# Long-row transposing DMAs with strided reads, a scale moved into the drive term, and a busier TensorE at the start

## The chip, the cores and the metric

The kernel runs on one core of one Trainium2 chip. The metric is the device time of that core in microseconds, from runs without a profile unless it is said otherwise. A run more than 1.5% above the fastest of the same kernel is called slow.

## The reference

The input is x and f_logit of shape (4, 6144, 256) and a `lower_bound` of 256 numbers. A gated recurrence runs along the tokens of each of the 4 sequences, and a maxout layer follows on all 24,576 tokens.

```python
sig = 1.0 / (1.0 + np.exp(-f_logit))
f = lower_bound + (1.0 - lower_bound) * sig
i = 1.0 - f
for t in range(S):
    h = f[:, t] * h + i[:, t] * x[:, t]
    y[:, t] = h
# y as (24576, 256); w1, w2: (256, 1024); w_out: (1024, 256)
out = np.maximum(y @ w1, y @ w2) @ w_out
```

The kernel uses max(a, b) = a + relu(b - a): it multiplies y by wd = w2 - w1 (1024 wide), applies a Relu, multiplies by w_out, and adds y times the fused matrix w13 = w1 @ w_out. Numbers are bf16 in SBUF.

## The kernel before

Tokens are worked on in blocks of 512 (48 blocks). For the recurrence, channels lie on partitions (two halves, KC = 2) and tokens along the free dimension. From the fifth chunk on (chunks of 1024 tokens = 2 blocks) the input is cast to bf16 into a DRAM scratch by GpSimd's DMA queue, and a transposing DMA on SP's queue brings it into SBUF:

```python
    def cross(c):
        nt = chunks[c][2]
        for s in range(2):                       # s = 0: f_logit, s = 1: x
            if by_xbar(c, s):                    # c >= 4
                dst = inpool.tile([P, KC, CH], BF16, name=("fT", "xT")[s])
                nc.sync.dma_start_transpose(
                    out=dst[:, :, 0:nt], in_=held[c, s][0:nt, :]
                )
                held[c, s] = dst
```

The gate runs on ACT (ScalarE): u = sigmoid(-f_logit). The rest of the recurrence runs on DVE (VectorE), in the order of this list (shortened: allocations and the lookup of the inputs are left out):

```python
    def gate(j):                                 # ACT
        nc.scalar.activation(out=like(u[:, :, 0:nb], fT), in_=fT,
                             func=AF.Sigmoid, scale=-1.0)

    def scan_steps(j):                           # DVE
        def decay(h):                            # ff = 1 - (1 - lower_bound) * u
            nc.vector.tensor_scalar(out=ff[:, h, 0:nb], in0=u[:, h, 0:nb],
                scalar1=nom[:, h : h + 1], scalar2=1.0, op0=ALU.mult, op1=ALU.add)
        def drive():                             # v = u * x; its factor om is folded into wd and w13
            nc.vector.tensor_tensor(out=like(v[:, :, 0:nb], xT),
                in0=like(u[:, :, 0:nb], xT), in1=xT, op=ALU.mult)
        def scan(h):                             # y[t] = ff[t] * y[t-1] + v[t]
            nc.vector.tensor_tensor_scan(out=y[:, h, 0:nb], data0=ff[:, h, 0:nb],
                data1=v[:, h, 0:nb], initial=init, op0=ALU.mult, op1=ALU.add)
        return [lambda: decay(0), lambda: decay(1), drive, lambda: scan(0), lambda: scan(1)]
```

The main loop interleaves the work of three neighbouring blocks. In the traces ACT and DVE run their instructions in the order in which they are issued here:

```python
        for j in range(2, NBLK + 1):
            ...
            gates = {}
            if j + 1 < NBLK and by_xbar(blocks[j + 1][3], 0):
                gates[0] = j + 1                 # gate of the NEXT block, after this block's first Relu
            if j + 2 < NBLK and not by_xbar(blocks[j + 2][3], 0):
                gates[FC // 2] = j + 2
            ...
            for fc in range(FC):                 # FC = 8
                if j < NBLK:
                    first_layer(j, fc)           # PE: 2 matmuls 128x512; ACT: Relu out of PSUM
                if j > 2:
                    second_layer(j - 1, fc)      # PE: 5 matmuls 128x256; at fc = 3 and 7 DVE evicts osb<-psO
                ...
                if fc in gates:
                    gate(gates[fc])
                if fc == 0 and 2 < j < NBLK - 1:
                    scans = scan_steps(j + 1)
                if fc < len(scans):
                    scans[fc]()
```

## Time and profile before

| | |
|---|---|
| time, median of the first 3 runs | 400.97 us (400.66 to 401.63) |
| span of the profiled run | 428.3 us, a slow run (430.05 us) |
| TensorE per block of 512 tokens, unstalled | 7.82 us |

These lines are from the page of before: the span, the busy time of each engine, TensorE's and DMA's busy tenths in 40 slices of the span (PE is TensorE, PEld its loading of weights, POOL is GpSimd), the DMA queue of SP (packets, MB, share of 16 engines' time), and the two lines of the chain that ended last.

```profile
span 428.3 us, 6970 instructions
PE 392.8 (92%) x2744; PEld 296.8 (69%) x2792; DVE 248.7 (58%) x359; ACT 268.5 (63%) x447; POOL 26.4 (6%) x58
...
PE   3999979798789999998997899999998999999996
...
DMA  7999999999999999999998999999999999998112
...
q1 hardware_dynamic: 100512, 51.13, 66.7%
...
PE 46%; DMA 34%; SPq 15%; ACT 3%; DVE 1%; issue 1%; ACTq 0%
PE psO L410 25%; DMA fT<-scr_0_90 20%; PE dT L381 19%; SPq L153 13%; DMA fT<-scr_1_91 12%; ACT u L190 2%; DMA w1n_110<-in_moe_w_dram 2%; SPq L433 1%; PE psO L352 1%; ACT rt L389 1%; PE tT L180 1%; PE psO L365 0%; SPq L121 0%; DVE osb L430 0%; DVE y L233 0%
```

In this slow run DMA is busy throughout and the chain runs through transposing DMAs. Between their stalls the blocks follow each other every 7.82 us (start of the first Relu of each block), and the stalls add up to 28.1 us. Without them the span is 400.2 us. The fast timed runs of before in the later rounds have spans of 398.6 to 400.2 us (a time is 1.8 us longer than its span). So fast runs should be bound by TensorE.

The three groups that the change touches, from the list of groups by line with shapes (busy us, mean ns of one | idle of the engine before, and who ended it):

```profile
L190 ACT ACTIVATE u<-fT 128x1024 bf16<-128x1024 bf16 x44 | 46.4, 1054 | 35.5 <-DMA fT<-scr_1_91 18.2 <-DMA fT<-scr_0_90 17.3
L220 DVE TENSOR_TENSOR v<-u,xT 128x1024 bf16<-128x1024 bf16 x44 | 30.3, 688 | 3.8 <-DMA xT<-scr_0_92 1.8 <-DMA xT<-scr_1_93 1.7
L209 DVE TENSOR_SCALAR ff<-u,nom 128x512 bf16<-128x512 bf16 x94 | 29.0, 351 | 105.0 <-ACT u L190 105.0
```

And one unstalled block of the recurrence, from the timeline of before (start us, duration us, and in brackets how long the engine had been idle and on whom it waited):

```profile
141.53 1.05 ACT L190 ACTIVATE u<-fT 128x1024 bf16<-128x1024 bf16 x1
...
142.62 0.62 DVE L209 TENSOR_SCALAR ff<-u,nom 128x512 bf16<-128x512 bf16 x2 [1.38 <-ACT u L190]
143.15 0.69 DVE L220 TENSOR_TENSOR v<-u,xT 128x1024 bf16<-128x1024 bf16 x1
...
144.46 0.69 DVE L430 COPY osb<-psO 128x512 f32<-128x512 f32 x1 [0.62 <-PE psO L410]
...
145.06 2.45 DVE L233 TENSOR_TENSOR_SCAN y<-ff,y,v 128x512 bf16<-128x512 bf16 x2
```

Gate, decay, drive and scans stand one behind the other, with an eviction of the output (`osb`, a copy out of PSUM) between drive and scans. DVE is idle twice in this block.

### The profile page before, as it was taken

The numbers are of one execution on the slowest core, as the hardware profiler recorded it, in microseconds if no ns is written. First come the engines' busy times: TensorE is split into PE (matmuls) and PEld (weight loads), VectorE is DVE, ScalarE is ACT, GpSimd is POOL, SyncE is SP. The second block draws the span as 40 slices with busy tenths as digits, with TensorE's granted clock in tenths as the row PEclk, the third lists the DMA queues.
The fourth block names the chain that finished last, engine by engine and source line by source line (L and its number), as shares of the span: only waits on it lengthen the run. The fifth ranks groups of instructions, "written<-read, shape, count | busy, mean of one in ns | idle before, by whom it ended". The sixth has DMA issues, their size and how long they took to land.

```text
span 428.3 us, 6970 instructions
## 1 busy us (share of the span) xinstructions
PE 392.8 (92%) x2744; PEld 296.8 (69%) x2792; DVE 248.7 (58%) x359; ACT 268.5 (63%) x447; POOL 26.4 (6%) x58
## 2 busy tenths in 40 slices
PE   3999979798789999998997899999998999999996
PEld 1677756576557777776775577767676777777775
DVE  5785637455357566564653557657547656567551
ACT  3656656557366676675673666756657676776762
POOL 1400000000000000000000000000000000000000
PEclk9999999999989999999999699999999999999999
DMA  7999999999999999999998999999999999998112
GB/s 245 222 220 198 123 157 141 137 169 252 81 240 226 119 239 233 112 248 168 183 237 75 218 158 186 250 145 170 219 131 231 226 216 164 268 157 179 79 69 100
DMA packets 103377, 77.01 MB, mean 180 GB/s; under 512 B 93552, under 2 KB 94064, under 8 KB 102640
## 3 DMA queue, kind: packets, MB, share of 16 engines
q1 hardware_dynamic: 100512, 51.13, 66.7%
q0 software_dynamic: 2544, 25.17, 36.1%
q8 instruction: 22, 0.36, 0.4%
q10 hardware_dynamic: 288, 0.26, 0.2%
q14 instruction: 11, 0.09, 0.1%
HBM read 53.48 MB, written 48.23 MB: 237 GB/s over the span
## 4 chain that ended last, share of the span: by engine, by line
PE 46%; DMA 34%; SPq 15%; ACT 3%; DVE 1%; issue 1%; ACTq 0%
PE psO L410 25%; DMA fT<-scr_0_90 20%; PE dT L381 19%; SPq L153 13%; DMA fT<-scr_1_91 12%; ACT u L190 2%; DMA w1n_110<-in_moe_w_dram 2%; SPq L433 1%; PE psO L352 1%; ACT rt L389 1%; PE tT L180 1%; PE psO L365 0%; SPq L121 0%; DVE osb L430 0%; DVE y L233 0%
## 5 line engine op out<-in xcount | busy, mean ns | idle before, releaser
L389 ACT ACTIVATE rt<-dT 128x512 bf16<-128x512 f32 x384 | 219.2, 598 | 104.1 <-PE dT L381 100.0
L381 PE MATMUL dT<-y,wd 128*128 128x512 bf16 x720 | 219.5, 384 | 21.3 <-ACT rt L389 19.5
L410 PE MATMUL psO<-wob,rt 128*128 128x256 bf16 x1536 | 230.7, 274 | 2.7 <-issue 0.4
L410 PEld LDWEIGHTS <-rt 128*128 128x128 bf16 x1536 | 170.7, 114 | 41.4 <-issue 1.1
L233 DVE TENSOR_TENSOR_SCAN y<-ff,y,v 128x512 bf16<-128x512 bf16 x88 | 107.9, 1268 | 0.1
L430 DVE COPY osb<-psO 128x512 f32<-128x512 f32 x94 | 64.7, 690 | 59.0 <-PE psO L410 58.9
L381 PEld LDWEIGHTS <-wd 128*128 128x128 bf16 x768 | 75.8, 99 | 33.2 <-issue 24.6
L209 DVE TENSOR_SCALAR ff<-u,nom 128x512 bf16<-128x512 bf16 x94 | 29.0, 351 | 105.0 <-ACT u L190 105.0
L410 PE MATMUL psO<-w_109,y 128*128 128x256 bf16 x384 | 74.0, 275 | 0.0
L410 PEld LDWEIGHTS <-y 128*128 128x128 bf16 x384 | 43.4, 113 | 42.6 <-issue 3.5
L190 ACT ACTIVATE u<-fT 128x1024 bf16<-128x1024 bf16 x44 | 46.4, 1054 | 35.5 <-DMA fT<-scr_1_91 18.2
L220 DVE TENSOR_TENSOR v<-u,xT 128x1024 bf16<-128x1024 bf16 x44 | 30.3, 688 | 3.8 <-DMA xT<-scr_0_92 1.8
L98 POOL DMA_DIRECT2D scr_0_90<-in_f_logit_dram x11 | 5.4, 493 | 149.7 <-DMA fT<-scr_0_90 149.7
L98 POOL DMA_DIRECT2D scr_1_91<-in_f_logit_dram x11 | 5.3, 486 | 148.8 <-DMA fT<-scr_1_91 148.1
L233 DVE TENSOR_TENSOR_SCAN y<-ff,v 128x512 bf16<-128x512 bf16 x6 | 7.0, 1208 | 0.0
L98 POOL DMA_DIRECT2D scr_0_92<-in_x_dram x11 | 5.4, 488 | 18.7 <-DMA xT<-scr_0_92 16.9
L98 POOL DMA_DIRECT2D scr_1_93<-in_x_dram x11 | 5.3, 486 | 15.7 <-DMA xT<-scr_1_93 14.9
L190 ACT ACTIVATE u<-tT 128x1024 bf16<-128x1024 bf16 x3 | 3.2, 1058 | 4.3 <-PE tT L180 4.3
L352 PE MATMUL psO<-ident_f,w1n_110 128*128 128x128 f32 x8 | 1.9, 422 | 3.4 <-DMA w1n_110<-in_moe_w_dram 3.4
L341 ACT ACTIVATE wd<-wdf,om 128x128 bf16<-128x128 f32 (+1 forms) x6 | 2.2, 428 | 4.3 <-DVE wdf L333 4.3
L352 PEld LDWEIGHTS psO<-ident_f,w1n_110 128*128 128x128 f32 x8 | 1.6, 221 | 3.7 <-issue 3.7
L220 DVE TENSOR_TENSOR v<-u,tT 128x1024 bf16<-128x1024 bf16 x3 | 3.6, 1216 | 0.0
(49 smaller groups left out, 45.1 us busy)
## 6 DMA issues: line engine op xcount, KB each, us to landing
out_dram<-osb SPq DMA_DIRECT2D x47, 512.0 KB, 4.8
scr_0_90<-in_f_logit_dram POOLq DMA_DIRECT2D x11, 512.0 KB, 7.5
scr_0_92<-in_x_dram POOLq DMA_DIRECT2D x11, 512.0 KB, 12.4
scr_1_91<-in_f_logit_dram POOLq DMA_DIRECT2D x11, 512.0 KB, 7.9
scr_1_93<-in_x_dram POOLq DMA_DIRECT2D x11, 512.0 KB, 13.6
fn<-in_f_logit_dram POOLq DMA_DIRECT2D x3, 256.0 KB, 7.9
xn<-in_x_dram POOLq DMA_DIRECT2D x3, 256.0 KB, 8.6
w2n_112<-in_moe_w_dram SPq DMA_DIRECT2D x1, 512.0 KB, 6.5
```

Source lines behind the costliest of these rows:

```text
L98: nc.gpsimd.dma_start(out=scr[0:nt, :].rearrange("(p i) d -> p (i d)", p=P), in_=src.rearrange("(p i) d -> p (i d)", p=P),)
L153: nc.sync.dma_start_transpose(out=dst[:, :, 0:nt], in_=held[c, s][0:nt, :])
L180: nc.tensor.transpose(dst, src, ident[:])
L190: nc.scalar.activation(out=like(u[:, :, 0:nb], fT), in_=fT, func=AF.Sigmoid, scale=-1.0)
L209: nc.vector.tensor_scalar(out=ff[:, h, 0:nb], in0=u[:, h, 0:nb], scalar1=nom[:, h : h + 1], scalar2=1.0, op0=ALU.mult, op1=ALU.add,)
L220: nc.vector.tensor_tensor(out=like(v[:, :, 0:nb], xT), in0=like(u[:, :, 0:nb], xT), in1=xT, op=ALU.mult,)
L233: nc.vector.tensor_tensor_scan(out=y[:, h, 0:nb], data0=ff[:, h, 0:nb], data1=v[:, h, 0:nb], initial=init, op0=ALU.mult, op1=ALU.add,)
L352: nc.tensor.transpose(pt[:, kc, q, :], half(w1n, g)[:, kc, 2 * r + q], ident_f[:])
L381: nc.tensor.matmul(dT[:, 0:nb], lhsT=wd[:, kc, fc * P : (fc + 1) * P], rhs=y[:, kc, 0:nb], start=(kc == 0), stop=(kc == KC - 1),)
L389: nc.scalar.activation(out=rt[:, 0:nb], in_=dT[:, 0:nb], func=AF.Relu)
L410: nc.tensor.matmul(ps[:, r, :], lhsT=left, rhs=right, start=(s == 0 and (r == 0 or j == NBLK - 1)), stop=(s == n - 1 and (r == 1 or j == N ...
L430: nc.vector.tensor_copy(out=osb[:, 2 * g : 2 * g + 2, :], in_=ps[:])
```

## The change

The intent: give the transposing DMAs 16 long rows (64 consecutive tokens each, 32 KB) instead of 1024 short ones, to make them cheaper. The price is that the tokens land interleaved: token 64 r + i lies at place i, sub-place r, so gate and drive read one token every 64 bytes. The scale om moves from the weights into the drive term, which saves work before the first matmul, and idle transposes are to keep TensorE's clock up at the start.

```diff
@@ cross, turn_steps
-                dst = inpool.tile([P, KC, CH], BF16, name=("fT", "xT")[s])
+                dst = inpool.tile([P, CH // XR * KC, XR], BF16, name=("fT", "xT")[s])
+                ni = nt // XR                                   # XR = 16
                 nc.sync.dma_start_transpose(
-                    out=dst[:, :, 0:nt], in_=held[c, s][0:nt, :]
-                )
-                held[c, s] = dst
+                    out=dst[:, 0 : ni * KC, :],
+                    in_=held[c, s][0:nt, :].rearrange("(r i) d -> r (i d)", r=XR),
+                )
+                held[c, s] = dst[:, 0 : ni * KC, :].rearrange(
+                    "p (i k) r -> p k r i", k=KC
+                )
...
-                turned[j, s] = held[c, s][:, :, o : o + nb]
+                ni = chunks[c][2] // XR
+                turned[j, s] = held[c, s][:, :, o // ni : (o + nb) // ni, :]
@@ the drive (also in the first recurrence)
+    def scaled_product(v, u, xT):
+        for h in range(KC):
+            nc.vector.scalar_tensor_tensor(
+                out=v[:, h], in0=u[:, h], scalar=om[:, h : h + 1], in1=xT[:, h],
+                op0=ALU.mult, op1=ALU.mult,
+            )
...
-            nc.vector.tensor_tensor(out=like(v[:, :, 0:nb], xT), in0=like(u[:, :, 0:nb], xT), in1=xT, op=ALU.mult)
+            scaled_product(like(v[:, :, 0:nb], xT), like(u[:, :, 0:nb], xT), xT)
@@ the weights: wd = w2 - w1 in one DVE subtract; om is no longer multiplied in
-        for kc in range(KC):
-            (nc.scalar.mul or nc.vector.tensor_scalar_mul of wdf by om)      # shortened
@@ the start
-        for q in range(8):
-            nc.tensor.transpose(wt[:, 0:P], ident[:], ident[:])
+        keep_busy(20)
...
         first_turn(1)
+        keep_busy(28)
         first_recurrence(1)
...   (first layer of block 0 before the transposes of w1; two w1T copies go to ACT)
```

More of the change, by code (lines that the diff above doesn't have):

```diff
@@ L38 @@
     CH = 1024
+    XR = 16
     assert S % CH == 0
@@ L197, in like @@
             return t
-        return t.rearrange("p k (m i) -> p k m i", m=P)
+        return t.rearrange("p k (m i) -> p k m i", m=src.shape[2])
+    def scaled_product(v, u, xT):
+        for h in range(KC):
+            nc.vector.scalar_tensor_tensor(
+                out=v[:, h],
+                in0=u[:, h],
+                scalar=om[:, h : h + 1],
+                in1=xT[:, h],
+                op0=ALU.mult,
+                op1=ALU.mult,
+            )
     def scan_steps(j):
@@ L219, in drive @@
             xT = turned[j, 1]
-            nc.vector.tensor_tensor(
-                out=like(v[:, :, 0:nb], xT),
-                in0=like(u[:, :, 0:nb], xT),
-                in1=xT,
-                op=ALU.mult,
-            )
+            scaled_product(like(v[:, :, 0:nb], xT), like(u[:, :, 0:nb], xT), xT)
         def scan(h):
@@ L272, in first_recurrence @@
             )
-        nc.vector.tensor_tensor(
-            out=like(v[:, :, cols], xT), in0=like(u[:, :, cols], xT), in1=xT,
-            op=ALU.mult,
-        )
+        scaled_product(like(v[:, :, cols], xT), like(u[:, :, cols], xT), xT)
         for h in range(KC):
@@ L300 @@
     wob = wpool.tile([P, FC, D], BF16)
-    wdf = wpool.tile([P, KC, DFF], FP32)
     wd = wpool.tile([P, KC, DFF], BF16)
@@ L333, in make_wd @@
         nc.vector.tensor_tensor(
-            out=wdf[:, :, cols].rearrange("p kc (q m) -> p kc q m", q=n),
+            out=wd[:, :, cols].rearrange("p kc (q m) -> p kc q m", q=n),
             in0=half(w2n, g)[:, :, qs],
@@ L338, in make_wd @@
         )
-        for kc in range(KC):
-            if g == 0:
-                nc.scalar.mul(wd[:, kc, cols], wdf[:, kc, cols], om[:, kc : kc + 1])
-            else:
-                nc.vector.tensor_scalar_mul(
-                    out=wd[:, kc, cols], in0=wdf[:, kc, cols], scalar1=om[:, kc : kc + 1]
-                )
     def turn_w1(k):
@@ L355, in turn_w1, with keep_w1T @@
         return pt
-    def keep_w1T(k, pt):
+    def keep_w1T(k, pt, copy):
         dst = w1T[:, 2 * k : 2 * k + 2, :].rearrange("p q (k d) -> p k q d", k=KC)
-        nc.vector.tensor_copy(out=dst, in_=pt[:])
+        copy(out=dst, in_=pt[:])
     def make_w13():
@@ L371, in make_w13, with keep_busy @@
                 )
-            nc.scalar.mul(w13[:, kc, :], psw[:, 0, :], om[:, kc : kc + 1])
+            nc.scalar.copy(out=w13[:, kc, :], in_=psw[:, 0, :])
+    def keep_busy(n):
+        wt = ps_d.tile([P, TB], BF16, name="dT")
+        for q in range(n):
+            nc.tensor.transpose(wt[:, 0:P], ident[:], ident[:])
     rts = {}
@@ L465 @@
         nc.scalar.activation(out=warm[:], in_=om[:, 0:1], func=AF.Sigmoid)
-        wt = ps_d.tile([P, TB], BF16, name="dT")
-        for q in range(8):
-            nc.tensor.transpose(wt[:, 0:P], ident[:], ident[:])
+        keep_busy(20)
         first_bf16(0, 0, nc.vector.tensor_copy)
@@ L479 @@
         make_wd(2, 2)
+        for fc in range(0, 4):
+            first_layer(0, fc)
         pts = [turn_w1(0), turn_w1(1)]
-        for fc in range(2):
+        make_wd(4, 2)
+        make_wd(6, 2)
+        for fc in range(4, 6):
             first_layer(0, fc)
         for k in range(2):
-            keep_w1T(k, pts[k])
-        for fc in range(2, 4):
+            keep_w1T(k, pts[k], nc.scalar.copy)
+        for fc in range(6, 8):
             first_layer(0, fc)
-        make_wd(4, 2)
-        make_wd(6, 2)
         pts = [turn_w1(2), turn_w1(3)]
-        for fc in range(4, 8):
-            first_layer(0, fc)
         for k in range(2):
-            keep_w1T(2 + k, pts[k])
+            keep_w1T(2 + k, pts[k], nc.vector.tensor_copy)
         make_w13()
```

## The prediction

> **What bounds the kernel now.** TensorE, from about 40 us on. In the timeline an unstalled block of 512 tokens takes 7.82 us (eight times two 128x512 matmuls and five 128x256, 0.977 us). ACT needs 8 x 0.60 + 1.05 = 5.9 us of it, DVE 2 x 0.35 + 0.69 + 2 x 1.27 + 2 x 0.69 = 5.3 us. The page's span, 428.3 us, is not the timed 401: the profiled run was a slow one. Its blocks lose 28.1 us to stalls, in which the gate waited for a transposed fT (list of waits: ACT from DMA fT 35.5 us); transposes and stores keep SP's queue full and the DMA row reads 9. 428.3 - 28.1 = 400.2 us, within 1 us of the timed median. So I believe that timed runs hardly stall: about 40.7 us of start, 45 blocks at 7.82, 8 us of end.
>
> **What the change does.**
> 1. Transposes from 16 rows of 32 KB. Today each has 2048 packets of 256 B (median 18 ns, mean 35 ns) and holds SP's queue 7 to 8 us, 2.2 at least. I expect fewer or cheaper packets and shorter issues. This takes away the profiled stalls (page span 400 to 410 us), but nearly nothing of the timed 401.
> 2. Reads with a stride of 64 B in gate and drive. The Trainium skill ("SBUF - State Buffer", note on cachelines) says that each access to a new 16-byte line pays a penalty; no read here shows it. Strided PSUM reads by the gate cost nothing (1058 ns against 1054). I estimate the gate at 1.05 to 1.9 us.
> 3. Drive as two scalar_tensor_tensor. The PSUM-fed drive takes 1.22 us for 1024 elements, so I estimate 2 x 0.62 us against 0.69: DVE 5.9 of 7.82 us. The scan ends 1.6 us before the next block and DVE waits 0.6 us for an eviction between drive and scans, which hides it. Not on the chain.
> 4. Start. wd needs one DVE subtract, no scaling: first matmul at about 11.8 instead of 12.93 us. The clock was half until 17.1 us ("TensorE: Matmul & The Clock Gate", Part 1: about 3.4 us of sustained work release it; the trace agrees: half clock from 119.5 to 122.9 us after a 4 us stall). Warm, 8 matmuls at 213 instead of 427 ns save 1.7 us of PE. But Relus (0.51 to 0.60 us each), the weights' landing (about 13.7 us), two w1T copies now in ACT's order (0.6 us each) and two on DVE (0.65 us) then decide when the fused weight matrix is done: by hand 20.8 us instead of 21.26. So 0.5 of a possible 2.5 us reaches the chain; the recurrences of blocks 1 and 2 follow unchanged.
>
> **Prediction.** 400.2 us, 397.5 to 402.5; faster by over 2%: 0.06, within 2%: 0.88, slower: 0.06.
>
> **What would show it.** Right: blocks 7.82 us apart; ACT's wait for DMA fT under 10 us; transposes issued in 2 to 4 us; drive near 2 x 0.62 us; block 0's first-layer matmuls 0.22 us apart, but block 3's first Relu still near 40 us. Wrong in step 1: transposes as long, or more packets. Wrong in step 4: block 3 before 39 us.
>
> **What would make it wrong.** Strided SBUF reads costing three times a plain one: DVE passes 7.82 us a block (slower). Transposes that read rows 32 KB apart more slowly, so that DMA bounds timed runs too. Or timed runs that do stall on DMA today behind a shorter start, which I cannot see; then the gain is 3 to 8 us.

## The result, and the profile after

| | before | after |
|---|---|---|
| time, median | 401.3 us of 4 runs, one of them slow (435.82) | 435.74 us of 4 runs (434.5 to 436.8) |
| ratio of fast runs | | 1.0863 (1.082 to 1.0905) |
| block to block | 7.82 us | 8.60 us |
| block 3's first Relu | 40.74 us (slow profile) | 40.95 us |

A ratio is the mean time of one kernel's fast runs over that of the other's in the same rounds, so not quite the ratio of the medians quoted. The changed kernel is 8.6% slower. Its loss is even: from block 3 to block 47 there are 44 steps of 8.60 instead of 7.82 us, 34.1 us in all, against 34.4 us between the medians.

The same lines of the page of after:

```profile
span 434.5 us, 7093 instructions
PE 396.6 (91%) x2784; PEld 298.9 (69%) x2832; DVE 301.1 (69%) x402; ACT 300.9 (69%) x443; POOL 26.6 (6%) x58
...
PE   6899998999899999989998999899989989998996
...
DMA  7998987897878679778788579798788877551212
...
q1 hardware_dynamic: 11104, 51.13, 40.0%
...
DVE 55%; ACT 21%; PE 12%; issue 8%; DMA 2%; SPq 1%; ACTq 0%; DVEq 0%
DVE y L245 24%; DVE v L208 20%; ACT u L196 20%; PE dT L387 7%; DVE osb L436 6%; PE psO L416 4%; DVE ff L226 4%; DMA w1n<-in_moe_w_dram 2%; ACT rt L395 2%; PE tT L186 1%; SPq L122 0%; PE psO L353 0%; DVE w1T L360 0%; PE psO L366 0%; ACTq L39
```

SP's queue has 11,104 packets instead of 100,512, and ACT does not wait for a transposed tile (what of this is owed to the state of before's profile, e8 below tells). But the chain has moved to DVE and ACT, though neither is busy for more than 69% of the span. That is the mark of a loop of latencies: no engine is full, and yet each waits for the one before. The groups:

```profile
L196 ACT ACTIVATE u<-fT 128x1024 bf16<-128x1024 bf16 x44 | 85.7, 1949 | 0.0
L208 DVE SCALAR_TENSOR_TENSOR v<-u,om,xT 128x512 bf16<-128x512 bf16 x88 | 92.5, 1093 | 0.0
L226 DVE TENSOR_SCALAR ff<-u,nom 128x512 bf16<-128x512 bf16 x94 | 29.0, 350 | 112.1 <-ACT u L196 112.1
```

The gate went from 1054 to 1949 ns, and the drive from one instruction of 688 ns to two of 1093 ns. The decay, whose operands are still contiguous, stayed. The chain of waits of after for one block, in order of time (start us, us, what):

```profile
170.47 1.94 ACT u L196
172.41 0.03 issue
172.44 0.04 DVE ff L226
172.48 0.23 issue
172.71 0.35 DVE ff L226
173.05 2.02 DVE v L208 x2
175.07 0.60 DVE osb L436
175.67 2.38 DVE y L245 x2
178.05 0.04 issue
178.09 0.39 PE dT L387
...
178.56 0.06 ACT rt L395
178.62 0.43 issue
179.06 1.95 ACT u L196
```

It closes on itself after 179.06 - 170.47 = 8.59 us. The gate of block j+1 stands in ACT's order behind the first Relu of block j; that Relu needs a matmul, which needs y of block j, whose scans need the drive and decay of block j, which need the gate of block j. Every term of this sum is a latency that all others wait for.

### The profile page after: what moved, and what is told of

It reads as the page before. It is cut to its first block, busy times and chain, and to the rows that moved or that the text cites. A ratio compares the mean times of both kernels' runs of the same rounds, so it can differ in the third digit from the quotient of the medians.

```text
span 434.5 us, 7093 instructions
## 1 busy us (share of the span) xinstructions
PE 396.6 (91%) x2784; PEld 298.9 (69%) x2832; DVE 301.1 (69%) x402; ACT 300.9 (69%) x443; POOL 26.6 (6%) x58
## 3 DMA queue, kind: packets, MB, share of 16 engines
q1 hardware_dynamic: 11104, 51.13, 40.0%
## 4 chain that ended last, share of the span: by engine, by line
DVE 55%; ACT 21%; PE 12%; issue 8%; DMA 2%; SPq 1%; ACTq 0%; DVEq 0%
DVE y L245 24%; DVE v L208 20%; ACT u L196 20%; PE dT L387 7%; DVE osb L436 6%; PE psO L416 4%; DVE ff L226 4%; DMA w1n<-in_moe_w_dram 2%; ACT rt L395 2%; PE tT L186 1%; SPq L122 0%; PE psO L353 0%; DVE w1T L360 0%; PE psO L366 0%; ACTq L395 0%
## 5 line engine op out<-in xcount | busy, mean ns | idle before, releaser
L387 PE MATMUL dT<-y,wd 128*128 128x512 bf16 x720 | 224.2, 382 | 28.4 <-DVE y L245 27.1
L208 DVE SCALAR_TENSOR_TENSOR v<-u,om,xT 128x512 bf16<-128x512 bf16 x88 | 92.5, 1093 | 0.0
L196 ACT ACTIVATE u<-fT 128x1024 bf16<-128x1024 bf16 x44 | 85.7, 1949 | 0.0
L387 PEld LDWEIGHTS <-wd 128*128 128x128 bf16 x768 | 75.2, 98 | 11.8 <-issue 2.5
L416 PE MATMUL psO<-w,y 128*128 128x256 bf16 x384 | 73.2, 272 | 0.0
L99 POOL DMA_DIRECT2D scr<-in_f_logit_dram x22 | 10.8, 490 | 286.1 <-DMA fT<-scr 285.4
L99 POOL DMA_DIRECT2D scr<-in_x_dram x22 | 10.7, 487 | 37.6 <-DMA xT<-scr 35.3
L378 PE MATMUL dT<-ident 128*128 128x128 bf16 x48 | 5.5, 314 | 1.6 <-DVE ident L455 1.6
L378 PEld LDWEIGHTS <-ident 128*128 128x128 bf16 x48 | 5.1, 150 | 1.6 <-DVE ident L455 1.6
L208 DVE SCALAR_TENSOR_TENSOR v<-u,om,tT 128x512 bf16<-128x512 bf16 (+1 forms) x10 | 5.9, 637 | 0.2 <-PE tT L142 0.2
L341 DVE TENSOR_TENSOR wd<-w2n,w1n 128x512 bf16<-128x512 f32 (+1 forms) x5 | 4.2, 888 | 0.7 <-DMA w1n<-in_moe_w_dram 0.7
```

The lines of the kernel that those rows point to most:

```text
L99: nc.gpsimd.dma_start(out=scr[0:nt, :].rearrange("(p i) d -> p (i d)", p=P), in_=src.rearrange("(p i) d -> p (i d)", p=P),)
L196: nc.scalar.activation(out=like(u[:, :, 0:nb], fT), in_=fT, func=AF.Sigmoid, scale=-1.0)
L208: nc.vector.scalar_tensor_tensor(out=v[:, h], in0=u[:, h], scalar=om[:, h : h + 1], in1=xT[:, h], op0=ALU.mult, op1=ALU.mult,)
L341: nc.vector.tensor_tensor(out=wd[:, :, cols].rearrange("p kc (q m) -> p kc q m", q=n), in0=half(w2n, g)[:, :, qs], in1=half(w1n, g)[:, :, qs],
L378: nc.tensor.transpose(wt[:, 0:P], ident[:], ident[:])
L387: nc.tensor.matmul(dT[:, 0:nb], lhsT=wd[:, kc, fc * P : (fc + 1) * P], rhs=y[:, kc, 0:nb], start=(kc == 0), stop=(kc == KC - 1),)
```

## The experiments

The theory: the time of a block is the larger of TensorE's 7.82 us and the sum along this loop. In the block of after shown above the terms, from start to start, are: gate 1.97, decay 0.53, drive 2.01 (the two instructions overlap a little; 2.10 from first start to last end), eviction 0.60, then scans, matmul and Relu 3.48, together 8.59. With the gate and drive of before (1.09 and 0.61 where DVE has no wait after it) the sum would be 6.31 us, hidden under 7.82 with 1.51 us to spare. The strided gate takes 0.88 of that and the new drive 1.40, together 2.28, which is 0.77 too much: 8.59. The rivals: the engines' throughput (DVE or ACT full through strides), the two-instruction drive in itself, or something in the long-row DMAs.

Block spacings below are medians of the start-to-start times of the blocks' first Relus in each run's trace.

### e1 and e8: the old transposes back, everything else changed

```diff
 (the changed kernel)
-  out=dst[:, 0 : ni * KC, :], in_=held[c, s][0:nt, :].rearrange("(r i) d -> r (i d)", r=XR)
+  out=dst[:, :, 0:nt], in_=held[c, s][0:nt, :]          # and the plain slice in turn_steps
```

> The changed kernel with the transposes and reads of before; the scaled drive and the new start stay. Theory (a latency loop closed by the strided reads: gate +0.90 us and drive +1.41 us against 1.53 us of slack): blocks back at 7.82 us, drive near 1.25 us as two instructions without a stride, time 399.5 to 402. Rival (the two-instruction drive and the longer DVE time are what costs): blocks stay over 8.2 us, time over 418.

Measured: 402.21, 432.1, 433.31 and 837.25 us. The profile is of the 837 us run, in which TensorE never got its full clock:

```profile
span 835.4 us, 7141 instructions
...
L382 PE MATMUL dT<-y,wd 128*128 128x512 bf16 x768 | 434.8, 677 | 0.2 <-DVE wd L336 0.2
```

Its blocks are 16.8 us apart with TensorE busy 99%. Its 512-column matmuls start 443 ns apart, against 216 ns at full clock and 427 ns at the half clock of other starts. The kernel was run again on another chip:

> The same kernel as e1 again, whose four runs fell at 402, 432, 433 and 837 us. If the 432 us runs are the slow state of the old transposes (the profiled run of before, 430 us), runs at 401 to 403 and at 430 to 436 come back, and blocks of a slow profile are 7.82 us but for stalls in which ACT waits for a transposed fT. Rival (the new drive or start costs): all runs over 428 with blocks evenly longer.

Measured: 400.49 us (400.34 to 401.29), ratio 0.9994 (0.9977 to 1.0011), blocks 7.82 us apart, drive 2 x 746 ns. Its profile is of a fast run with the old transposes: ACT never waits for fT, and the median issue of a transpose takes 2.6 us. So the scaled drive in two instructions, without a stride, and the whole new start cost nothing; they gain nothing measurable either. The loss is in the layout. The runs at 432 and 433 us did not come back in e8, so what made them is not settled by this pair (see the end of this section).

### e2: the layout alone, in the kernel before

```diff
 (the kernel before, with only the hunks "cross, turn_steps" of the change)
```

> The kernel before with only the long-row transposes and the strided reads; the drive stays one tensor_tensor, the start as before. Theory: gate 1.95 us, drive about 2.1 us for 1024 elements, blocks 8.5 to 8.7 us apart, time 430 to 438. Rival: without the scaled drive most of the loss is gone, under 412.

Measured: 427.46 us, ratio 1.0656 (1.064 to 1.0672), blocks 8.41 us. The range was missed on the low side, because one tensor_tensor with a stride takes 1914 ns and not 2.1 us. The loop explains the size: from drive to eviction it is 1.84 instead of 2.01 us, and 8.59 - 0.17 = 8.42. So most of the loss needs nothing but the strides. A stride also takes away the cheaper drive: 688 ns became 1914.

### e3 and e4: one strided operand each

```diff
 (the changed kernel; LONG = 0 in e3, LONG = 1 in e4)
+                if s == LONG:      # long rows and strided reads
...
+                else:              # old transpose, contiguous reads
```

> The changed kernel with long rows for f_logit only: strided gate (1.95 us), plain drive (about 1.25 us). Theory: gate +0.90 and drive +0.55 us stay just under the 1.53 us of slack, so blocks 7.82 to 7.9 us and 400 to 405. Rival (each strided engine costs its share, by throughput or by port contention): about 0.3 us a block, 413 to 420.

> The changed kernel with long rows for x only: plain gate (1.05 us), strided drive (2 x 1.09 us). Theory: drive +1.41 us alone is under the slack of 1.53 us, blocks 7.82 us, 400 to 403. Rival (each strided engine costs its share): about 0.48 us a block, 420 to 425.

Measured: e3 404.27 us, ratio 1.0092 (1.0065 to 1.012), blocks 7.91 us, gate 1949 ns, drive 2 x 746 ns. e4 403.73 us (400.57 to 407.63, the last one slow), ratio 1.0005 (0.9976 to 1.0033), blocks 7.82 us, gate 1052 ns, drive 2 x 1092 ns. The groups, first of e3 and then of e4:

```profile
L207 ACT ACTIVATE u<-fT 128x1024 bf16<-128x1024 bf16 x44 | 85.8, 1949 | 0.0
L219 DVE SCALAR_TENSOR_TENSOR v<-u,om,xT 128x512 bf16<-128x512 bf16 x88 | 62.0, 746 | 0.0
```

```profile
L207 ACT ACTIVATE u<-fT 128x1024 bf16<-128x1024 bf16 x44 | 46.3, 1052 | 0.0
L219 DVE SCALAR_TENSOR_TENSOR v<-u,om,xT 128x512 bf16<-128x512 bf16 x88 | 92.5, 1092 | 3.5 <-DMA xT<-scr 3.5
```

The ratio of e4 also leaves out its profiled run of 405.59 us; with it the ratio would be 1.004. Four blocks of that profile are longer than 7.82 us, by 5.0 us together, and DVE waits 3.5 us for transposed x, so at least part of it is a stall by DMA and not an even loss.

This is the sharpest pair. Each half of the strides alone costs little (e4 0.1%, or 0.4% with the run left out; e3 0.9%), and both cost 8.6%. A throughput or contention cost would have been shared out. The sums give both spacings: e3 has the drive at 1.32 us instead of 2.01, 8.59 - 0.69 = 7.90, just over TensorE's 7.82; e4 has the gate at 1.09 instead of 1.97, 8.59 - 0.88 = 7.71, under it.

### e5: the gate taken out of the loop

Nothing is made faster. The gate of block j+2 is issued half way through block j, so that no Relu of block j+1 stands before it.

```diff
-            if j + 1 < NBLK and by_xbar(blocks[j + 1][3], 0):
-                gates[0] = j + 1
-            if j + 2 < NBLK and not by_xbar(blocks[j + 2][3], 0):
+            if j + 2 < NBLK:
                 gates[FC // 2] = j + 2
```

> The changed kernel, strides and all, with one difference: the gate of block j+2 is issued on ACT half way through block j, as it is for the first blocks, instead of the gate of block j+1 at the start of block j. Theory (the time of a block is the sum along the loop from scan to matmul to Relu to gate to decay to drive to scan): the gate leaves the loop, nothing gets faster, DVE stays near 6.5 us of work a block, and blocks are 7.82 us apart, TensorE-bound: 400 to 403 us, ACT's gate still 1.95 us, drive still 2 x 1.09 us. Rival (throughput of DVE and ACT, slowed by strides): nothing is taken away, so blocks stay over 8.4 us and the time over 428.

Measured: 402.17 us (402.11 to 406.27), ratio 1.0055 (1.0017 to 1.0093), blocks 7.82 us. Gate and drive are as slow as in after (1963 and 1097 ns). The busy times of a middle stretch of 63 us, first of after and then of e5, from the windows view (length, then busy us and count of PE, PEld, DVE, ACT and POOL, then TensorE's clock, DMA share, GB/s):

```profile
130.00:193.00 63.00, 58.24 (x407) 43.75 (x413) 46.11 (x61) 45.66 (x67) 3.89 (x8) 1.00 0.79 177
```

```profile
130.00:193.00 63.00, 63.00 (x453) 47.95 (x452) 50.49 (x65) 50.34 (x73) 3.89 (x8) 1.00 0.88 203
```

In e5 DVE works 50.5 of 63 us and ACT 50.3, more than in after, and TensorE is full. So DVE and ACT had room in after, and the rival of throughput falls. The long-row DMAs are all still there, so they fall as a rival too. The remaining loss is at the start: block 3's first Relu comes at 40.9 us, against 39.2 us in e8's fast profile, as the first strided gate now stands among the Relus of block 2. The spans of these two profiles, 400.3 and 398.6 us, differ by the same 1.7 us.

### e10: the eviction taken out of the loop

```diff
-                if fc < len(scans):
-                    scans[fc]()
+                if scans:      # decay, decay at fc = 0; drive at 1; both scans at 2: before the eviction of fc = 3
+                    for k in {0: (0, 1), 1: (2,), 2: (3, 4)}.get(fc, ()):
+                        scans[k]()
```

> The changed kernel with one difference: DVE runs the two scans straight after the drive, and evicts the first half of the output after them. Nothing is removed or made faster. Theory (the loop of a block is a sum of latencies, in which the eviction between drive and scans has 0.6 us): blocks 8.0 us instead of 8.60, 408 to 411 us. Rival (throughput of DVE and ACT): no change, 434 to 437 us.

Measured: 408.61 us (408.36 to 410.49), ratio 1.0201 (1.0175 to 1.0228; unclear as a verdict at 2% against before, clear against after), blocks 8.00 us. The timeline of e10 shows the scans straight behind the drive and both evictions after them:

```profile
152.09 1.96 ACT L196 ACTIVATE u<-fT 128x1024 bf16<-128x1024 bf16 x1
...
154.61 2.11 DVE L208 SCALAR_TENSOR_TENSOR v<-u,om,xT 128x512 bf16<-128x512 bf16 x2
156.64 2.45 DVE L245 TENSOR_TENSOR_SCAN y<-ff,y,v 128x512 bf16<-128x512 bf16 x2
159.01 1.26 DVE L436 COPY osb<-psO 128x512 f32<-128x512 f32 x2
160.11 1.96 ACT L196 ACTIVATE u<-fT 128x1024 bf16<-128x1024 bf16 x1
```

Moving 0.60 us of unchanged work out of the loop makes it 8.59 - 0.60 = 7.99 us and gains 27 us of the run. The same instructions run as in after.

### e6: runs read, strides written

The gate reads the transposed tile in runs of 8 tokens (16 bytes) and leaves u interleaved; decay and drive read runs and write with a stride of 128 bytes into token order.

```diff
-                    "p (i k) r -> p k r i", k=KC
+                    "p (i k) r -> p k i r", k=KC
...   (gate: u kept as "p k (i r)"; decay and drive: out viewed as "p k (r i) -> p k i r")
```

> The changed kernel with its order of access turned round: the gate reads the transposed tile in runs of 8 tokens (16 bytes) and leaves u interleaved; decay and drive read runs and write with a stride of 128 B into token order. If what costs is a read that meets a new 16-byte line for each element and writes are free: gate back to about 1.05 us, decay 0.35 to 0.6 us, drive 2 x 0.75 us, blocks 7.82 to 8.0 us, 400 to 409 us. If strided writes cost as much as strided reads: decay and drive about 1.1 us for each 512, blocks about 9 us, 445 to 465 us.

Measured: 594.38 us, ratio 1.4818, blocks 12.16 us; the result is correct. Both branches of the expectation missed the size. The groups of e6:

```profile
L215 DVE SCALAR_TENSOR_TENSOR v<-u,om,xT 128x512 bf16<-128x512 bf16 x88 | 221.1, 2710 | 0.0
L235 DVE TENSOR_SCALAR ff<-u,nom 128x512 bf16<-128x512 bf16 x88 | 112.2, 1476 | 71.8 <-ACT u L196 71.8
...
L196 ACT ACTIVATE u<-fT 128x1024 bf16<-128x1024 bf16 x44 | 46.2, 1050 | 0.0
```

The gate is back at 1050 ns from the same tile, read in runs of 16 bytes: so its extra time in after is the order of its reads, not the tile or the DMA. On DVE the writes with a stride of 128 bytes are dearer than the reads with one of 64 bytes: the decay went from 350 to 1476 ns, the drive to 2710. The loop gives this spacing too: medians of 1.08 us from gate to decay, 2.15 on to the drive, 4.63 to the eviction, 0.83 to the scans and 3.47 to the next gate make 12.16, with DVE busy for 55.0 us of a stretch of 63. Why the drive takes longer still than the decay was not separated; it has the same strided output and two inputs read in runs.

### e7, e9 and e11: towards a version that keeps the long rows

e7 is e5 with 40 instead of 28 idle transposes. e9 is e5 with the first strided gate (block 4) issued behind the last Relu of block 2. e11 has both.

```diff
-        keep_busy(28)
+        keep_busy(40)                       # e7, e11
...
+            if j + 2 < NBLK and j > 2:      # e9, e11
+                gates[FC // 2] = j + 2
+            if j == 2:
+                gates[FC - 1] = j + 2
```

> As e5 with 40 instead of 28 idle transposes before the first layer, so that TensorE works without a gap from 7.8 us until the first weights are ready. Theory: full clock from 11 to 14.6 us instead of sometimes 15.9, but Relus, weight arrival and the fused weight matrix decide the start, so within 1 us of e5. Rival: the start is bound by TensorE at half clock, then 1 to 2 us less than e5.

> As e5, but the first gate that reads a transposed tile (block 4) is issued after the last Relu of block 2 instead of half way through it, where it cost e5 1.8 us (block 3's first Relu at 40.9 instead of 39.2 us). Theory: blocks 7.82 us as in e5, block 3 near 39.2 us, 400.2 to 400.9 us, level with fast runs of before or up to 0.2% under them, and none of its runs over 410, as the long-row transposes leave DMA time. Rival: the long rows and strides cost something beyond the loop, so it stays at 402 or over.

> e9 with 40 instead of 28 idle transposes. e9's profile got the full clock only at 15.8 us, as the changed kernel's did, and its block 1 began 1.7 us later than that of e5, e7, e8 and e10, whose full clock came between 9.7 and 11.9 us. Theory: with no gap before the first weights the full clock always comes by about 12.5 us, so block 1 near 26.5 us, block 4 near 47.4 us, and 400.2 to 401.0 us in all runs, level with fast runs of before or a little under. None over 410. Rival: the start does not depend on it and it stays at 402 to 403.

Measured: e7 402.37 us (402.17 to 402.92), ratio 1.0036; no gain over e5, as expected. e9 402.26 us (400.86 to 404.2), ratio 1.0030; the expectation missed. Its profile shows the full clock only at 15.8 us, block 1 at 28.1 us and block 4 at 49.0 us. e11 401.00 us (400.9 to 401.33), ratio 1.0002 (0.9988 to 1.0016): the full clock at 11.8 us, block 1 at 26.7 us and block 4 at 47.6 us. Moving the first gate did save time in both: from block 2 to block 4 e5 takes 13.3 us, e9 and e11 12.0 and e8 11.6; in the profile of e9 the late clock hides it. e11 is level with the fast runs of before, and 34.7 us better than the change. No version that clearly beats fast runs of before was found, and none was to be expected: blocks of 7.82 us are TensorE's, and only the first 40 us and the last 8 are left.

### What stays open: the slow runs

Of the 44 timed runs of before, over all rounds and without the profiled one of 430.05 us, 8 were slow (414 to 443 us). Of the 38 runs of the eight kernels with long rows for both inputs, none was. Before's slow profile shows ACT waiting for transposed tiles and DMA full, and long rows take some DMA time away, so it is plausible that they remove that state; but no experiment provoked or removed it, and e1 and e8, the same kernel, differ. It stays a count. Over all 11 runs of before in e11's rounds the mean is 407.15 us, against 401.05 us of e11's six; this mean includes slow runs.

## Why the prediction was wrong

- **The bound of before: right.** TensorE at 7.82 us a block, fast runs without stalls. No fast run of before has a trace, but e8 and e11 run at exactly that spacing.
- **Step 1, the DMAs: fewer packets, but little gained in fast runs.** The transposes' 90,112 packets of 256 bytes became 704 of 32 KB. The other marks that I named read as right only against before's slow profile: SP's issue of a transpose fell there from 7 to 8 us to about 3, and ACT's wait for fT from 35.5 us to nothing. In e8, a fast run with the old transposes, the issue has a median of 2.6 us (3.0 in e11) and ACT doesn't wait for fT either. What is left, between two fast runs of like length, is the share of SP's queue: 51.3% in e8 against 45.7% in e11. "Nearly nothing of the timed 401" holds.
- **Step 2, the strides: half applied.** The gate was put at "1.05 to 1.9 us" and measured 1.95. For the drive, which reads with the same stride, step 3 took the time of the PSUM-fed drive, "2 x 0.62 us", and left the stride out. It measured 2 x 1.09 us, of which the two instructions without a stride (2 x 0.75 us in e8) are harmless. This is the term of the sum that was mis-sized.
- **Step 3, the drive at "2 x 0.62 us" and "Not on the chain": the step that failed.** I allowed the drive 0.55 us more than before. With its stride it took 1.40 us more (2.01 instead of 0.61 us from its start to DVE's next instruction). With the gate's 0.88 that makes 2.28 us against a slack of 1.6 us by my count and 1.51 by the sums, so the path that I called hidden set the pace, 8.60 us a block. Charging both costs together would not have been enough: with my own sizes, at most 0.85 for the gate and 0.55 for the drive, the sum of 1.40 still fits, and e3, whose drive has no stride, runs at 7.91 us a block. But I did not form the sum either; I held the drive alone against the slack. The strided drive alone fits, the strided gate with a plain drive nearly does, and both do not (e4, e3, after). I also counted "DVE waits 0.6 us for an eviction" as a further cushion. In after that wait is gone, and the eviction itself, 0.60 us of work, stands in the loop (e10).
- **"What would make it wrong" asked for the wrong quantity.** It named strided reads so dear that "DVE passes 7.82 us a block". DVE's work in after is 0.70 + 2.19 + 2.54 + 1.35 = 6.8 us a block (from the means of its groups; busy for 6.3, as neighbours overlap), well under 7.82, and e5 shows that the same work fits. What passed 7.82 us was the sum along a loop over ACT, DVE and TensorE.
- **Step 4, the start: the small size was right, the mechanism only in part.** In after's profile the clock was full only at 15.9 us, in spite of 28 idle transposes from 7.8 to 11.0 us, and block 0's matmuls were still 0.43 us apart. A gap of 1.2 us followed before the first weights were ready. Six other profiled kernels with those same 28 transposes (e3, e4, e5, e6, e8, e10) got it between 9.7 and 12.0 us, e9 at 15.8 and e1's odd run never. With the clock early, block 1's first Relu comes at 26.4 to 26.8 us, late at 28.1 to 28.2. In the time it is lost in the noise: e8 against before, 0.9994.

The Trainium skill was used at three points. "SBUF — State Buffer" (Door 1: The DMA port swizzle, the note on cachelines) says that SBUF has lines of 16 bytes and that each access to a new one pays. The trace agrees: 1949 ns for 1024 elements 64 bytes apart, 1050 in runs of 16 bytes. That the boundary lies at 16 bytes no run here shows. I quoted the page and then used it for one reader of two. "TensorE: Matmul & The Clock Gate" (Wait — 56ns, not 53.3ns?) gives N / 2.4 + 2.5 ns between warm matmuls; two of 512 and five of 256 columns make 978 ns by it (an estimate), and the trace has 0.977 us, so 7.82 us is the pace of warm TensorE. The same page (What's actually happening) says that the clock is released by a free-running window of about 3.4 us, so that the moment varies by ±500 ns. Here it varied more: in eight profiles with the same start it came between 9.7 and 12.0 us six times and at 15.8 and 15.9 us twice. The page's figure is for matmuls back to back, and this start has gaps; no run separates why.

## What to carry to other kernels

When several engines pass a recurrence around, write down the loop that closes on itself, with the start-to-start time of each step, and charge every added cost to its one slack together; costs that each fit can fail in sum. An engine's busy share does not show such a loop, while a chain of waits that repeats with the period of a block does. Before undoing a change that lengthened such a loop, look for an instruction in it that need not be there: issuing the gate earlier, with not one instruction faster, won back 33.6 us.

## What the Trainium skill lacked or had wrong

- "SBUF — State Buffer", the note on cachelines, gives no size for the penalty. Reads of bf16 elements 64 bytes apart: ACT 1949 against 1054 ns for 128x1024; DVE scalar_tensor_tensor with one strided input 1093 against 746 ns for 128x512; tensor_tensor 1914 against 688 ns for 128x1024.
- "VectorE: DVE Perf Modes" (Mode 1× (REGULAR) — the baseline) says that "weird strides" work in this mode and gives one result a cycle, without a price for the stride. The 1093 ns against 746 above show one; in which mode these instructions ran, no run shows. Strided writes are on no page read for this: a stride of 128 bytes on the output took tensor_scalar from 350 to 1476 ns, and scalar_tensor_tensor from 746 to 2710.
- "DMA: Bandwidth & Descriptors" (DMA Transpose (X-bar)) does not say that the shape of the rows sets the packets: 1024 rows of 512 bytes gave 2048 packets of 256 bytes in a transposing DMA, the same bytes as 16 rows of 32 KB gave 16 packets of 32 KB (704 for 44 DMAs). In fast runs the share of SP's queue went from 51.3% (e8) to 45.7% (e11); its issue time did not fall (medians 2.6 and 3.0 us).
- "TensorE: Matmul & The Clock Gate" (What's actually happening) puts the ramp at less than 1% of a typical kernel's span. One run of e1 never got its full clock: 512-column matmuls 443 ns apart to its end, 837 us against 402, with TensorE busy 99%; the mean clock given for that run was 1.0 and its record has no entry of a clock at all. It was seen once and is unexplained. The nearest thing on the page is its warning (Seeing it yourself) of a clock stuck at a quarter for over 50 us.
